# Eight matmuls without a reader, three between gate and up and five between up and w_down

## The chip, the cores and the metric

The kernel runs on one core of one Trainium2 chip. The metric is device time in microseconds (us); a kernel's time is the median of its runs. One more execution is taken with the hardware profiler, and all durations of single instructions come from that one.

## The reference

One decode step of a transformer block for two sequences (B = 2, one token each, D = 640): a modulation of two layer norms by a condition vector, an attention over a cached window, and a gated feed-forward part.

```python
mod = (silu(c) @ w_mod).reshape(2, 6, 1, 640)        # sa, ca, ga, sb, cb, gb
h = layernorm(x) * (1 + ca) + sa
# attention: 32 heads of 192, the last 1024 rows of the caches
q = (h @ wq).reshape(2, 1, 32, 192).transpose(0, 2, 1, 3)
p = softmax(einsum('bhqd,bhkd->bhqk', q, k) * 192 ** -0.5)
o = einsum('bhqk,bhkd->bhqd', p, v)
x = x + ga * (o.transpose(0, 2, 1, 3).reshape(2, 1, 6144) @ wo)
# feed-forward part, F = 1536
h = layernorm(x) * (1 + cb) + sb
return x + gb * ((gelu(h @ w_gate) * (h @ w_up)) @ w_down)
```

All inputs are bf16. The caches and the weights are read once.

## The kernel before

Two rows of activations meet some 77 MB of weights and caches, so the program is one long stream of loads on the SP queue, in an order written out by hand: w_mod, wq, four loads of the key cache, four of the value cache (three places in SBUF hold them in turn), then wo in two pieces, w_gate, w_up and w_down in two pieces of 10 and 2 of its 12 row tiles (`WD_SPLIT`). A load waits only until its place is free.

Every engine gets its instructions as a list in program order. `S.op` and `S.dma` record an operation with what it reads and writes; `emit` writes each list out and puts a semaphore wait before an instruction whose producers run on another engine. TensorE runs its list strictly in that order.

The products with weights are laid out in four column groups: the row block is held as a 128x32 tile, and four matmuls, for the four quarters of the output columns, go to four strips of the array and write to four 32-partition strips of one PSUM bank. So a `wo`, `gate`, `up` or `down` product is a run of matmuls in groups of four: 192 for wo (L577, 128 after the first piece of wo has landed and 64 after the second), 20 each for gate and up (`ffn_gu`, L593), 48 for w_down (L611, 40 and 8 by the two pieces).

The tail of the program, from wo on, is a chain:

- wo (TensorE, L577), its scaling by `ga` and the residual sum (VectorE, L582 and L584);
- the second layer norm (L331 to L354) and the transposition of its result to `hT` (L324);
- `ffn_gu` for gate into bank `BK_G[0]` = 5 (waits for `hT` and w_gate), the gelu on ScalarE (L599);
- `ffn_gu` for up into bank 6 (waits for w_up), the product `geglu` on VectorE (L602), its transposition to `aT` (L324);
- down (TensorE, L611; its first matmul waits for `aT` and the first piece of w_down, its 41st for the second piece);
- the scaling by `gb` and the residual sum (L617, L619), and the store.

`warm(n, bk)` is a helper that the kernel already uses in the scores of the key cache, four matmuls a step (`NF`) into bank 4. It issues `n` matmuls of the 128x128 identity with the 128x384 tile `qbc` (the queries, set early in the program) into a bank that nobody reads afterwards. The first of them (L425) loads the weights, the others (L418, in `held`) keep them:

```python
for i in range(n):
    put = e.matmul if i == 0 else lambda *a, **k: held(e, *a, **k)
    last = put(ps[:, bk, 0:2 * Dh], lhsT=ident_b[:, :], rhs=qbc[:, :, :].rearrange("p b d -> p (b d)"),
               start=True, stop=True)
```

`MB` is (7, 4): the banks of the two halves of the modulation. Bank 7 is read for the last time by the copy of the first half (`mod0_evac`, L372), at the start of the program.

Of the kernel before, what the change touches and what calls it, by code (L numbers as in the profile page):

```python
# [103 lines left out]
def bass_adaLN_cond__sliding_block_cached__geglu_ffn__decode_kernel(  # L104
# [62 lines left out]
    with es:  # L167
# [69 lines left out]
        def bank(k):  # L237
            return ("bank", k)
# [119 lines left out]
        MB = (7, 4)  # L358
# [55 lines left out]
        def held(e, out, lhsT, rhs, start, stop):  # L414
            i = mybir.InstMatmult(name=nc.get_next_instruction_name(), engine=mybir.EngineType.PE,
                                  ins=[e.lower_ap(rhs), e.lower_ap(lhsT)], outs=[e.lower_ap(out)],
                                  start_tensor_calc=start, stop_tensor_calc=stop, tile_size=(P, P), tile_position=(0, 0), ldweights=False)
            return e.add_instruction(i)  # L418

        def warm(n, bk):  # L420
            def f(e):
                last = None
# [4 lines that stand above are left out]
                return last  # L427
            S.op("pe", f, reads=["ident_b", "qbc"], writes=[bank(bk)], name="warm")
# [159 lines left out]
        def ffn_gu(bk, wv, key, name, ka, kb):  # L588
            def f(e):
                last = None  # L590
                for k in range(ka, kb):
                    for j in range(NJ):
                        last = e.matmul(ps[SQ * j:SQ * j + SQ, bk, 0:FN], lhsT=hT[:, k, :], rhs=wv[:, k, FN * j:FN * j + FN],  # L593
                                        start=(k == 0), stop=(k == KT - 1), tile_position=(0, SQ * j), skip_group_check=True)
                return last
            S.op("pe", f, reads=["hT", key], writes=[bank(bk)], name="ffn_" + name)

        ffn_gu(BK_G[0], wg_v, "wg", "wg", 0, KT)
        S.op("act", lambda e: e.activation(out=gl, in_=ps[:, BK_G[0], 0:FN], func=ACTF.Gelu_apprx_tanh),  # L599
             reads=[bank(BK_G[0])], writes=["gl"], name="gelu")  # L600
        ffn_gu(BK_G[1], wu_v, "wu", "wu", 0, KT)
        S.op("dve", lambda e: e.tensor_tensor(out=aC[:, :], in0=ps[:, BK_G[1], 0:FN], in1=gl, op=ALU.mult),  # L602
             reads=[bank(BK_G[1]), "gl"], writes=["aC"], name="geglu")
        to_contraction(aT[:, :, :], aC[:, :], FT, ["aC"], ["aT"], "aT")
# [52 lines left out]
```

## Time and profile before

| | before |
|---|---|
| median of 3 runs | 187.43 us (187.03 to 187.66) |
| profiled execution: time / span | 187.47 us / 186.2 us |
| TensorE matmul busy | 110.8 us (59%), 921 instructions |
| VectorE busy | 101.2 us (54%) |
| load queue's share of the 16 DMA engines | 96.2% |
| read from HBM | 76.88 MB, 413 GB/s over the span |
| mean granted TensorE clock | 0.857 |

The span runs from the first to the last instruction of the profiled execution; 1.27 us of its time lie outside. PE is TensorE's matmuls, PEld its weight loads, DVE is VectorE, ACT ScalarE, SP the engine that issues the loads. The granted clock is the share of full speed that TensorE's throttle let through.

### The profile page before, as it was taken

The numbers are of one execution on the slowest core, as the hardware profiler recorded it, in microseconds if no ns is written. First come the engines' busy times: TensorE is split into PE (matmuls) and PEld (weight loads), VectorE is DVE, ScalarE is ACT, GpSimd is POOL, SyncE is SP. The second block draws the span as 40 slices with busy tenths as digits, with TensorE's granted clock in tenths as the row PEclk, the third lists the DMA queues.
The fourth block names the chain that finished last, engine by engine and source line by source line (L and its number), as shares of the span: only waits on it lengthen the run. The fifth ranks groups of instructions, "written<-read, shape, count | busy, mean of one in ns | idle before, by whom it ended". The sixth has DMA issues, their size and how long they took to land.

```text
span 186.2 us, 1823 instructions
## 1 busy us (share of the span) xinstructions
PE 110.8 (59%) x921; PEld 35.4 (19%) x697; DVE 101.2 (54%) x106; ACT 13.1 (7%) x22; POOL 5.0 (3%) x12
## 2 busy tenths in 40 slices
PE   0004500861089989998899986299759267184333
PEld 0001200330000000000000000256435145183113
DVE  6811500010586999999999994738393601103431
ACT  2002200032000000000000000200100001200300
POOL 8200000000000000000000000000000000000000
PEclk9999999997557999999999999859966969758555
DMA  7999999898998989899998989999898999999980
GB/s 264 396 449 488 475 436 396 348 500 380 465 475 370 487 359 496 370 475 443 412 468 370 496 359 486 412 443 475 363 486 370 465 422 417 418 413 416 426 339 11
DMA packets 2347, 76.99 MB, mean 413 GB/s; under 512 B 292, under 2 KB 292, under 8 KB 420
## 3 DMA queue, kind: packets, MB, share of 16 engines
q1 hardware_dynamic: 2316, 76.88, 96.2%
q8 instruction: 6, 0.10, 0.2%
q10 hardware_dynamic: 24, 0.01, 0.0%
q14 instruction: 1, 0.01, 0.0%
HBM read 76.88 MB, written 0.00 MB: 413 GB/s over the span
## 4 chain that ended last, share of the span: by engine, by line
DMA 44%; DVE 35%; PE 17%; SPq 1%; issue 1%; ACT 0%; DVEq 0%
DMA pp<-in_A_k_cache_dram 25%; DVE pp L432 19%; DMA pp<-in_B_w_down_dram 19%; PE ps L498 12%; DVE r L432 7%; DVE Sg L452 5%; PE ps L418 4%; DVE Em L483 2%; PE ps L611 1%; SPq L252 1%; PE ps L445 1%; DVE On L515 0%; DVE M L458 0%; ACT E_sb L472 0%; PE ps L467 0%
## 5 line engine op out<-in xcount | busy, mean ns | idle before, releaser
L432 DVE TENSOR_TENSOR pp<-pp,qbc 128x6144 bf16<-128x6144 bf16 x12 | 40.1, 3350 | 9.3 <-DMA pp<-in_A_k_cache_dram 9.3
L418 PE MATMUL ps<-pp,ident_b 128*128 128x512 bf16 x132 | 32.8, 400 | 0.0
L498 PE MATMUL ps<-pp,Em 128*64 128x384 bf16 x192 | 23.3, 419 | 9.8 <-DMA pp<-in_A_v_cache_dram 5.1
L483 DVE TENSOR_TENSOR Em<-E_sb,M32b 128x2048 bf16<-128x2048 bf16 x8 | 18.2, 2289 | 8.5 <-PE ps L498 7.8
L498 PEld LDWEIGHTS ps<-pp,Em 128*64 128x64 bf16 x192 | 14.0, 141 | 18.8 <-issue 5.4
L432 DVE TENSOR_TENSOR r<-r,qbc 128x6144 bf16<-128x6144 bf16 x4 | 13.4, 3349 | 0.0
L452 DVE TENSOR_REDUCE Sg<-ps 128x32 f32<-128x512 f32 x16 | 11.0, 685 | 4.4 <-PE ps L418 4.4
L367 PE MATMUL ps<-pp,scT 128*32 128x480 bf16 x40 | 4.4, 601 | 15.0 <-DMA pp<-in_w_mod_dram 15.0
L445 PE MATMUL ps<-pp,ident_b 128*128 128x512 bf16 x12 | 4.9, 407 | 13.4 <-DVE pp L432 13.4
L388 PE MATMUL ps<-r,hT 128*32 128x512 bf16 x60 | 5.5, 545 | 11.5 <-DMA r<-in_A_wq_dram 11.5
L418 PE MATMUL ps<-qbc,ident_b 128*128 128x384 bf16 x48 | 10.6, 330 | 0.0
L418 PE MATMUL ps<-r,ident_b 128*128 128x512 bf16 x44 | 10.1, 379 | 0.0
L399 DVE CAST qC<-ps 128x512 bf16<-128x512 f32 x1 | 0.7, 692 | 16.1 <-PE ps L388 16.1
L577 PE MATMUL ps<-r,oT 128*32 128x160 bf16 x192 | 5.7, 305 | 5.6 <-DMA r<-in_A_wo_dram 5.6
L425 PEld LDWEIGHTS ps<-qbc,ident_b 128*128 128x128 bf16 x16 | 1.6, 101 | 37.7 <-issue 37.7
L515 DVE TENSOR_SCALAR On<-ps,rden 32x192 bf16<-32x192 f32 x4 | 1.7, 418 | 12.4 <-PE ps L498 12.4
L577 PEld LDWEIGHTS ps<-r,oT 128*32 128x32 bf16 x192 | 5.2, 131 | 6.0 <-DMA r<-in_A_wo_dram 6.0
L472 ACT ACTIVATE E_sb<-Sg,nb 128x256 bf16<-128x256 f32 x2 | 1.0, 500 | 74.4 <-DVE nb L470 74.4
L582 DVE TENSOR_TENSOR lnt<-ps,modC 128x160 f32<-128x160 f32 x1 | 0.3, 325 | 10.7 <-PE ps L577 10.7
L593 PE MATMUL ps<-pp,hT 128*32 128x384 bf16 x40 | 3.6, 522 | 3.9 <-DVE hT L324 2.6
L425 PE MATMUL ps<-qbc,ident_b 128*128 128x384 bf16 x16 | 5.4, 338 | 0.7 <-ACT qbc L397 0.7
L445 PEld LDWEIGHTS ps<-pp,ident_b 128*128 128x128 bf16 x12 | 1.2, 97 | 24.4 <-DVE pp L432 23.3
(76 smaller groups left out, 66.0 us busy)
## 6 DMA issues: line engine op xcount, KB each, us to landing
pp<-in_A_k_cache_dram SPq DMA_DIRECT2D x3, 6144.0 KB, 41.4
pp<-in_A_v_cache_dram SPq DMA_DIRECT2D x3, 6144.0 KB, 21.7
r<-in_A_wq_dram SPq DMA_DIRECT2D x1, 7680.0 KB, 31.8
r<-in_A_k_cache_dram SPq DMA_DIRECT2D x1, 6144.0 KB, 38.9
r<-in_A_v_cache_dram SPq DMA_DIRECT2D x1, 6144.0 KB, 22.3
r<-in_A_wo_dram SPq DMA_DIRECT2D x1, 5120.0 KB, 28.7
pp<-in_w_mod_dram SPq DMA_DIRECT2D x1, 4800.0 KB, 14.1
r<-in_A_wo_dram SPq DMA_DIRECT2D x1, 2560.0 KB, 34.4
```

Of the source, the lines that this page charges most:

```text
L252: return lambda e: e.dma_start(dst, src)
L367: last = e.matmul(ps[SQ * j:SQ * j + SQ, bk, 0:3 * DN].rearrange("p (i n) -> p i n", i=3), lhsT=scT[:, k, :], rhs=wm_v[:, k, 3 * part * D: ...
L388: last = e.matmul(ps[SQ * j:SQ * j + SQ, BK_H + c, 0:QW], lhsT=hT[:, k, :], rhs=wq_v[:, k, RN * j + QW * c:RN * j + QW * (c + 1)], start=( ...
L418: return e.add_instruction(i)
L425: last = put(ps[:, bk, 0:2 * Dh], lhsT=ident_b[:, :], rhs=qbc[:, :, :].rearrange("p b d -> p (b d)"), start=True, stop=True)
L432: S.op("dve", lambda e: e.tensor_tensor(out=places[k][:, JH * q:JH * (q + 1), :], in0=places[k][:, JH * q:JH * (q + 1), :], in1=qbc[:, b, ...
L445: last = put(o_ap, lhsT=ident_b[:, :], rhs=places[k][:, JH * q:JH * (q + 1), ci * GC:(ci + 1) * GC], start=(ci == 0), stop=(ci == NCH - 1))
L452: S.op("dve", lambda e: e.tensor_reduce(out=S_sb[:, b, a:a + JH], in_=ps[:, q % 2, 0:JH * GC].rearrange("p (j c) -> p j c", j=JH), axis=AX ...
L483: S.op("dve", lambda e: e.tensor_tensor(out=Em[:, t % 2, :, :], in0=E_sb[:, b, J * t:J * (t + 1)].unsqueeze(2).broadcast_to([P, J, H]), in ...
L498: last = e.matmul(ps[r:r + 2 * H, BK_O[b], 0:ON], lhsT=Em[:, t % 2, 2 * jp:2 * jp + 2, :].rearrange("p j c -> p (j c)"), rhs=places[k][:, ...
L577: last = e.matmul(ps[SQ * j:SQ * j + SQ, BK_M, 0:DN], lhsT=oT[:, t, :], rhs=wo_v[:, t, DN * j:DN * j + DN], start=(t == 0), stop=(t == NT ...
L593: last = e.matmul(ps[SQ * j:SQ * j + SQ, bk, 0:FN], lhsT=hT[:, k, :], rhs=wv[:, k, FN * j:FN * j + FN], start=(k == 0), stop=(k == KT - 1) ...
```

## The change

One `warm` of three matmuls is put behind gate's matmuls and one of five behind up's, both into bank 7.

```diff
         ffn_gu(BK_G[0], wg_v, "wg", "wg", 0, KT)
+        warm(3, MB[0])
         S.op("act", lambda e: e.activation(out=gl, in_=ps[:, BK_G[0], 0:FN], func=ACTF.Gelu_apprx_tanh),
              reads=[bank(BK_G[0])], writes=["gl"], name="gelu")
         ffn_gu(BK_G[1], wu_v, "wu", "wu", 0, KT)
+        warm(5, MB[0])
         S.op("dve", lambda e: e.tensor_tensor(out=aC[:, :], in0=ps[:, BK_G[1], 0:FN], in1=gl, op=ALU.mult),
              reads=[bank(BK_G[1]), "gl"], writes=["aC"], name="geglu")
```

The lines behind it move by one or two (gelu L600, geglu L604, down L613, `gb` L619 and L621).

## The prediction, made before the changed kernel ran

> **What bounds the kernel now.** I read the page first: the row of the granted clock and the chain that ended last.
>
> ```profile
> PEclk9999999997557999999999999859966969758555
> ...
> DMA 44%; DVE 35%; PE 17%; SPq 1%; issue 1%; ACT 0%; DVEq 0%
> ```
>
> The loads run through nearly the whole span, and TensorE stands at half clock (5) in the last three slices, where the change is made. The chain in order of time, of the last 40 us, says what sets the end (start, duration, what):
>
> ```profile
> 146.36 35.41 DMA pp<-in_B_w_down_dram
> 181.78 0.14 issue
> 181.91 1.82 PE ps L611 x47
> ```
>
> The last large load, w_down, lands at 181.78. Behind it come down's matmuls, two small VectorE steps and the store; nothing overlaps them. So of TensorE's work in the tail only down's 1.8 us is on the path. The timeline of TensorE (start, duration, tile, what ended the idle time before) shows what stands ahead of it:
>
> ```profile
> 162.60 4.46 PE L577 MATMUL ps<-r,oT 128*32 128x160 bf16 x128 [3.91 <-DMA r<-in_A_wo_dram]
> 168.71 1.29 PE L577 MATMUL ps<-r,oT 128*32 128x160 bf16 x64 [1.64 <-DMA r<-in_A_wo_dram]
> ...
> 174.83 1.79 PE L593 MATMUL ps<-pp,hT 128*32 128x384 bf16 x20 [2.58 <-DVE hT L324]
> 177.99 1.79 PE L593 MATMUL ps<-pp,hT 128*32 128x384 bf16 x20 [1.37 <-DMA pp<-in_B_w_up_dram]
> 181.91 1.79 PE L611 MATMUL ps<-pp,aT 128*32 128x160 bf16 x48 [2.13 <-DMA pp<-in_B_w_down_dram]
> ```
>
> Gate is followed by a hole of 1.37 us, ended by w_up's landing; up by one of 2.13 us, ended by w_down's. In the second hole VectorE works (whole timeline):
>
> ```profile
> 179.90 0.56 DVE L602 TENSOR_TENSOR aC<-ps,Sg 128x384 bf16<-128x384 f32 x1 [5.13 <-PE ps L593]
> 180.50 0.85 DVE L324 STREAM_TRANSPOSE aT<-aC 128x384 bf16<-128x384 bf16 x1
> ```
>
> aT is done at 181.35, 0.43 us before w_down lands: that is up's slack.
>
> Last, the rule of the clock. In rows of a quarter microsecond it changes at 119.28, 126.08, 143.16, 149.99, 153.40, 160.23, 167.05 and 170.47, always a whole multiple of 3.41 us apart. So I cut the span on that grid (stretch, length, PE busy with its matmuls, granted clock, DMA share, GB/s):
>
> ```profile
> 136.33:139.74 3.41, 2.60 (x18) 0.50 1.07 461
> 139.74:143.16 3.42, 3.42 (x24) 0.50 1.00 431
> ...
> 149.99:153.40 3.41, 2.83 (x18) 0.50 0.97 420
> ...
> 163.64:167.05 3.41, 3.41 (x104) 0.50 0.94 401
> 167.05:170.47 3.42, 1.30 (x68) 1.00 1.01 424
> ...
> 173.88:177.29 3.41, 1.79 (x20) 0.50 1.01 428
> 177.29:180.71 3.42, 1.79 (x20) 0.50 0.90 371
> ```
>
> No stretch is mixed; each decides the clock of the next. A cold stretch with 2.83 us or more of busy TensorE was followed by full clock, one with 2.60 was not. A stretch at full clock with 2.32 or 2.04 kept it (143.16 and 112.43), one with 1.30 lost it. Before the change neither stretch ahead of down comes near: 1.79 and 1.79.
>
> **The change part by part.**
>
> Removed and moved: nothing. The order of the changed kernel's instructions shows ScalarE, VectorE and SP with the same lists, and the eight matmuls (plus two weight loads) on TensorE without a wait: `qbc` and the identity are old, bank 7 was last read near 18 us. gelu and geglu wait for gate's and up's own counts, so no reader waits for the new ones.
>
> Three matmuls behind gate: 384 columns each. Gate's 20 matmuls are five groups of four, 1.79 us with 0.19 us of run-out at the end, so 0.32 us a group; a 128x384 matmul that fills the array should take the same 0.32 us at half clock (L425's and L418's rows, 338 and 330 ns in the mean, mix clocks and run-out). They run from 176.43 to 176.43 + 3 x 0.32 = 177.39, to 177.58 with run-out. Up starts at 177.99. Cover: the wait for w_up, 0.4 us to spare; cost nothing. Their weight load adds between nothing and 0.1 us (L425's PEld, 96 to 151 ns); I take nothing, because at 57.18 the helper's first matmul followed the earlier group without a visible hole. Were the cover gone, up would start up to 0.96 + 0.1 us late, of which up's slack takes 0.43.
>
> Five behind up: from 179.59 for 1.60 us, to 181.19, 181.38 with run-out. down can't start before aT (181.35) and w_down (181.78). This cover doesn't depend on the load: geglu and aT take 1.45 us after up anyway. Cost nothing; bounds 0 and 0.1.
>
> What they do to the clock: the stretch 173.88 to 177.29 gets 174.83 to 177.29 = 2.46 us, under the 2.60 that didn't suffice. The stretch 177.29 to 180.71 gets 0.29 + (180.71 - 177.99) = 3.01 us (2.82 without the run-out in the hole, about the 2.83 that sufficed). So the clock rises at 180.71, before down.
>
> The grid may lie otherwise in another execution, so I ask for every position. Busy blocks are now 174.83 to 177.58 and 177.99 to 181.38. A stretch holds 2.83 us or more if it ends anywhere from 178.07 (start 174.66) to 181.91 (start 178.50). That interval is 3.84 us long, the grid 3.41: some boundary always falls in it, and the clock is up when down starts, unless a further boundary takes it back (second rival).
>
> The Trainium skill, "TensorE: Matmul & The Clock Gate", Part 1 ("What's actually happening"), calls the window free-running and not reset by a kernel's start; the grid above agrees on its length (3.41 us), and the one trace can't show whether it moves between executions.
>
> What a full clock saves: wo gives both prices for the same matmul (128x32 weights, 160 columns). At half clock 32 groups took 4.46 us: (4.46 - 0.19)/32 = 0.133 us a group. At full clock 16 groups took 1.29: (1.29 - 0.17)/16 = 0.070. down is 12 groups: cold 12 x 0.133 + 0.19 = 1.79, as its row says; warm 12 x 0.070 + 0.17 = 1.01. Saved: 0.78 us, all on the path. Bounds are 0 (no rise) and 0.78. The second piece of w_down doesn't become the new wait: the DMA share is 0.07 of an engine set at 182.0 to 182.1 and nothing by 182.2, and a warm down needs it after 181.91 + 10 x 0.070 = 182.61.
>
> Up running faster, where the clock rises early, gains nothing: w_down still lands at 181.78.
>
> Sum: 187.47 - 0.78 = 186.69 us. The profiled execution is 0.04 above the median of the runs.
>
> **The rivals.**
>
> *The clock doesn't rise in time: no change, 187.4.* For it: the margin is thin, 3.01 or 2.82 against a threshold between 2.60 and 2.83, and a hole between gate's matmuls and the helper's (their weight load) would take another 0.1. Against: two of the readings reach a level at which it did rise. The Trainium skill's same page and part (table of the two states) asks for a whole window of sustained activity, some 3.4 us; by it the longest unbroken block, 177.99 to 181.38 = 3.39 us, falls just short and the saving is 0. The row at 149.99 speaks against this reading: 2.83 of 3.41 us sufficed.
>
> *The clock rises early and falls back: between 186.7 and 187.4.* If a boundary lies between 178.07 and 179.6, up and the helper run at double pace (0.80 + 0.80 + 0.19 us), TensorE then stands still to 181.91, and the next boundary comes at 181.48 to 183.0, before or in down. That stretch holds some 1.8 us busy, between the 1.30 that lost the clock and the 2.04 that kept it. 1.5 of 3.41 positions are concerned; in a bit under half of these I expect a loss, of half the gain in the mean.
>
> *The three matmuls hold up back: slower, 188.1.* If gate ends later against w_up's landing (wo's last 64 matmuls at half clock would make it 16 x 0.063 = 1.0 us later), the three start at 177.43 and end at 178.39, up starts 0.4 late, which the 0.43 of slack just takes. It costs time from where gate is more than 1.0 us late, and in full (1.06 - 0.43 = 0.63 us) only where w_up and w_down both have landed before; and then the clock mustn't rise either. 187.47 + 0.63 = 188.1. The 1.37 us hole with DMA as its end speaks against it.
>
> **How the numbers follow.** Forecast 0.66, no rise 0.15, fall back 0.10, held back 0.06, the rest 0.03. About 0.3% (0.56 us) is what a measurement of this kernel tells from no change, so the forecast, 0.4%, counts as faster, mostly; a part of it measured short of 0.3% is set off by falls back that keep most of the gain. Faster 0.66; same takes the first two rivals, 0.25; slower the third and part of the rest, 0.09. The runs before spread by 0.4 us to either side of their median, so the forecast's own range is 186.3 to 187.1. The whole range must reach the case of no change: 186.2 to 187.5, which leaves the slower case out.
>
> **What would show it.** Right: in the profile after, three and five matmuls end before up and down start, up still waits for w_up and down for w_down at the same times, the clock reads 1.00 through down, and the 48 matmuls take about 1.0 us in place of 1.79. Wrong: down at 1.79 us with the clock at 0.50 (no rise), down with a change of pace inside (fall back), up starting at the end of the three matmuls (held back), or a down that is fast while the end doesn't come earlier.

## The result

The changed kernel takes 186.88 us (median of 13 runs, 186.72 to 187.36) against 187.51 (13 runs, 186.81 to 187.81): ratio 0.997, 95% interval 0.996 to 0.998. That is 0.63 us, just over the 0.3% (0.56 us) that can be told from no change. The profiled execution took 186.95 us with a span of 185.7, against 187.47 and 186.2.

First TensorE's part of the timeline of the changed kernel (start, duration, engine, line, tile; what ended the idle time before):

```profile
168.77 2.32 PE L577 MATMUL ps<-r,oT 128*32 128x160 bf16 x64 [1.64 <-DMA r<-in_A_wo_dram]
...
175.93 1.79 PE L593 MATMUL ps<-pp,hT 128*32 128x384 bf16 x20 [2.58 <-DVE hT L324]
177.66 0.50 PE L425 MATMUL ps<-qbc,ident_b 128*128 128x384 bf16 x1
177.95 0.85 PE L418 MATMUL ps<-qbc,ident_b 128*128 128x384 bf16 x2
178.73 1.79 PE L593 MATMUL ps<-pp,hT 128*32 128x384 bf16 x20
180.45 0.50 PE L425 MATMUL ps<-qbc,ident_b 128*128 128x384 bf16 x1
180.74 1.35 PE L418 MATMUL ps<-qbc,ident_b 128*128 128x384 bf16 x4
182.15 1.01 PE L613 MATMUL ps<-pp,aT 128*32 128x160 bf16 x48
```

down's 48 matmuls take 1.01 us, before 1.79. But up starts at 178.73, before at 177.99, and without a wait for a load: it starts where the three helpers end. wo's last 64 matmuls took 2.32 us here, before 1.29. The chain that ended last shows the consequence: it no longer goes through w_down's landing.

```profile
177.72 0.43 PE ps L425
178.16 0.64 PE ps L418 x2
178.80 1.75 PE ps L593 x12
...
181.24 0.87 DVE aT L324
182.11 0.04 issue
182.15 1.04 PE ps L613 x48
```

Two of the helpers' rows and up are links of the chain now, and down waits for aT (182.10). Cut at this execution's own clock boundaries (stretch, length, PE busy, granted clock, DMA share, GB/s):

```profile
175.00:178.42 3.42, 2.49 (x23) 0.50 1.00 425
178.42:181.83 3.41, 3.41 (x27) 0.50 0.69 277
181.83:185.24 3.41, 1.28 (x50) 1.00 0.01 5
```

The grid lies elsewhere than before (181.83 against 180.71). The stretch of up and the five is wholly busy, and the clock rises 0.32 us ahead of down.

The sum of this execution: 0.78 us won in down, 182.15 - 181.91 = 0.24 lost in its later start, 0.54 in all; the two profiled times differ by 0.52.

The single runs of before say more than their median. For 78 of them, made beside the experiments below, the mean granted clock of each run is on record. In 67 it is 0.855 to 0.872, and all of these take 187.24 us or more; in the other 11 it is 0.874 to 0.883, and they take 186.51 to 187.36. So before, too, some executions seem to reach the time of the changed kernel, with a higher clock. None of these was profiled, so that down ran at full clock in them is not shown.

### The profile page after: what moved, and what is told of

It reads as the page before. It is cut to its first block, busy times and chain, and to the rows that moved or that the text cites. A ratio compares the mean times of both kernels' runs of the same rounds, so it can differ in the third digit from the quotient of the medians.

```text
span 185.7 us, 1833 instructions
## 1 busy us (share of the span) xinstructions
PE 110.3 (59%) x929; PEld 35.9 (19%) x699; DVE 101.4 (55%) x106; ACT 13.1 (7%) x22; POOL 4.8 (3%) x12
## 4 chain that ended last, share of the span: by engine, by line
DMA 45%; DVE 36%; PE 16%; issue 1%; SPq 1%; ACT 0%; DVEq 0%
DMA pp<-in_A_k_cache_dram 25%; DMA r<-in_A_wo_dram 19%; DVE pp L432 19%; DVE r L432 7%; PE ps L498 7%; DVE Sg L452 5%; PE ps L418 4%; PE ps L593 2%; PE ps L577 1%; DVE Em L483 1%; SPq L252 1%; PE ps L613 1%; PE ps L445 1%; DVE aT L324 0%; DVE M L458 0%
## 5 line engine op out<-in xcount | busy, mean ns | idle before, releaser
L418 PE MATMUL ps<-pp,ident_b 128*128 128x512 bf16 x132 | 32.0, 393 | 0.0
L498 PE MATMUL ps<-pp,Em 128*64 128x384 bf16 x192 | 20.2, 379 | 14.2 <-DMA pp<-in_A_v_cache_dram 12.9
L367 PE MATMUL ps<-pp,scT 128*32 128x480 bf16 x40 | 4.4, 601 | 15.1 <-DMA pp<-in_w_mod_dram 15.1
L388 PE MATMUL ps<-r,hT 128*32 128x512 bf16 x60 | 6.0, 586 | 11.5 <-DMA r<-in_A_wq_dram 11.5
L418 PE MATMUL ps<-qbc,ident_b 128*128 128x384 bf16 x54 | 12.6, 346 | 0.0
L445 PE MATMUL ps<-pp,ident_b 128*128 128x512 bf16 x12 | 4.9, 407 | 12.8 <-DVE pp L432 12.8
L577 PE MATMUL ps<-r,oT 128*32 128x160 bf16 x192 | 6.8, 339 | 5.1 <-DMA r<-in_A_wo_dram 5.1
L577 PEld LDWEIGHTS ps<-r,oT 128*32 128x32 bf16 x192 | 6.1, 146 | 5.5 <-DMA r<-in_A_wo_dram 5.5
L425 PE MATMUL ps<-qbc,ident_b 128*128 128x384 bf16 x18 | 6.2, 345 | 0.7 <-ACT qbc L397 0.7
L388 PEld LDWEIGHTS ps<-r,hT 128*32 128x32 bf16 x60 | 2.4, 140 | 15.4 <-issue 15.3
```

The lines of the kernel that those rows point to most:

```text
L367: last = e.matmul(ps[SQ * j:SQ * j + SQ, bk, 0:3 * DN].rearrange("p (i n) -> p i n", i=3), lhsT=scT[:, k, :], rhs=wm_v[:, k, 3 * part * D: ...
L388: last = e.matmul(ps[SQ * j:SQ * j + SQ, BK_H + c, 0:QW], lhsT=hT[:, k, :], rhs=wq_v[:, k, RN * j + QW * c:RN * j + QW * (c + 1)], start=( ...
L445: last = put(o_ap, lhsT=ident_b[:, :], rhs=places[k][:, JH * q:JH * (q + 1), ci * GC:(ci + 1) * GC], start=(ci == 0), stop=(ci == NCH - 1))
L498: last = e.matmul(ps[r:r + 2 * H, BK_O[b], 0:ON], lhsT=Em[:, t % 2, 2 * jp:2 * jp + 2, :].rearrange("p j c -> p (j c)"), rhs=places[k][:, ...
L577: last = e.matmul(ps[SQ * j:SQ * j + SQ, BK_M, 0:DN], lhsT=oT[:, t, :], rhs=wo_v[:, t, DN * j:DN * j + DN], start=(t == 0), stop=(t == NT ...
```

## The experiments

Theory 1: TensorE's clock for a stretch of 3.41 us is set by how long it was busy in the stretch before; the eight matmuls lift that over a threshold. Theory 2: all that counts is that TensorE is busy right ahead of down. Theory 3: the three hold up back in some executions and cost part of the gain. Runs of one group below share their runs of before.

**One half of the change at a time**

```diff
-        warm(3, MB[0])      # five_only
-        warm(5, MB[0])      # three_only
```

> The three matmuls behind gate are left out, the five behind up stay. Theory 1 (the clock): a stretch of the 3.41 us grid must hold about 2.83 us of busy TensorE. The block from 177.99 to 181.38 is then alone, and a stretch must end between 180.82 and 181.91 to have down at full clock from its start: a third of all positions. Where it ends up to 1 us later, a part of down is fast; in the other third there is no gain. So times scatter between 186.7 and 187.5, the mean gains 0.3 to 0.45 us, less than the change's 0.63. Theory 2 (what counts is only that TensorE is busy right ahead of down): the whole 0.63 us, as with all eight, and no more scatter.

> The five behind up are left out, the three behind gate stay. Theory 1: gate, three and up give at most 2.75 + a part of 1.79 in a row, so for some positions a stretch from about 174.7 to 178.1 or 176 to 179.8 rises, but then TensorE stands still from 179.8 to 181.9 and the clock may fall back: mean gain 0 to 0.2, median about 0. Theory 2: no gain. Theory 3 (the three hold up back by up to 0.7 us where wo's second part runs at half clock, as the profile of the changed kernel shows): up to 0.3 us slower than before in those executions.

The five alone: 186.79 us, ratio 0.9978 (0.9964 to 0.9992). The twelve runs fall in two groups: eight from 186.53 to 186.90, four from 187.22 to 187.55; the mean gains 0.50 us (187.46 before, 30 runs), more than the 0.3 to 0.45 expected. Theory 2, which expects no more scatter than the change has, does not fit these four; what decides against it is a profile shown further down (as_changed). The mean granted clock of each run parts the groups as well: 0.878 to 0.890 in the eight, 0.863 to 0.872 in the four. (One stretch of 3.41 us at full instead of half clock makes 0.009 of a span of 186 us.) The profiled execution is of the good group, and its windows show why:

```profile
177.53:180.95 3.42, 3.19 (x25) 0.50 0.86 351
180.95:184.36 3.41, 1.24 (x49) 1.00 0.10 38
```

The boundary at 180.95 lies in the interval that the expectation named (180.82 to 181.91). The other group wasn't profiled; that its boundaries lie outside is argued, not shown. Eight good runs of twelve are also more than the third of all positions that the expectation gave them: it took every position for equally likely.

The three alone: 187.40 us, ratio 0.9989 (0.9974 to 1.0004), so not told from no change; the mean gains 0.20. Three of the twelve runs, at 186.64 to 186.74, are as fast as the change, which theory 1 allows for some positions; none of them was profiled. The profiled execution shows theory 3 without the gain:

```profile
178.67 1.79 PE L593 MATMUL ps<-pp,hT 128*32 128x384 bf16 x20
182.07 1.79 PE L612 MATMUL ps<-pp,aT 128*32 128x160 bf16 x48 [1.62 <-DVE aT L324]
```

Up starts at 178.67, behind the three, and down, at half clock, waits for aT to 182.07. The stretch ahead held too little for a rise (175.10 to 178.51: 2.64 us busy). This execution took 187.68 us, 0.16 over the median before.

**The same matmuls, a quarter of the array; and the change again**

```diff
-        warm(3, MB[0])
+        strip(3, MB[0])
...
-        warm(5, MB[0])
+        strip(5, MB[0])
# strip: each matmul with lhsT=ident_b[:, 0:SQ], out=ps[0:SQ, bk, 0:2 * Dh], tile_position=(0, 0)
```

> The same eight matmuls at the same places, 128x384 each, but with only 32 of the 128 columns of the weights, so that each fills one of four strips of the array and takes the same 0.32 us at half clock. Theory 1a (the clock follows the time that TensorE is busy): the gain of the change, 0.63 us, down at about 1.0 us. Theory 1b (it follows how much of the array works): the eight count a quarter, the stretches hold at most 1.8 + 0.4 us, down stays at 1.79 us, and the time is that of before or up to 0.3 us over it, where the three hold up back. This would also be the control for theory 2, which expects the gain of 0.63.

> The changed kernel once more, on the chip of the three others: 186.9 us, a gain of 0.6 us. Its profile shows another position of the clock's grid: if that is free against the kernel's start, the boundaries lie elsewhere than at 178.42 and 181.83. Where wo's last 64 matmuls take 1.3 us, up starts by w_up's landing near 178.0 and down by w_down's; where they take 2.3, up starts at the end of the three, near 178.7, and down by aT, near 182.1.

one_strip takes 186.69 us (7 runs, 186.62 to 186.75), ratio 0.9962 (0.9948 to 0.9977): the full gain, as theory 1a has it and 1b does not. A second profile of the same kernel (strip_again, below) shows the stretch ahead of the rise:

```profile
177.23:180.64 3.41, 3.08 (x26) 0.50 0.94 386
```

Up's 1.79 us are in it; the other 1.29 are strip matmuls alone. Counted as a quarter these would give 1.79 + 0.32 = 2.11 us, and no stretch at half clock with so little was followed by full clock. So the clock follows the time in which TensorE is busy, also where its matmuls use 32 of 128 columns.

The change again: 186.81 us (12 runs, 186.57 to 187.04), ratio 0.9968 (0.9957 to 0.9979). Its windows, and down:

```profile
175.43:178.84 3.41, 2.76 (x23) 0.50 0.99 420
178.84:182.26 3.42, 2.19 (x42) 1.00 0.57 224
...
182.03 1.02 PE L613 MATMUL ps<-pp,aT 128*32 128x160 bf16 x48 [1.23 <-DMA pp<-in_B_w_down_dram]
```

2.76 us sufficed. It is also the case that decides against theory 2: from 180.79 TensorE stood still for 1.23 us, waiting for w_down, and down still took 1.02.

The profiled execution of one_strip has the slow wo (2.33 us) too, and yet:

```profile
177.51 0.85 PE L434 MATMUL ps<-qbc,ident_b 128*32 128x384 bf16 x2
177.95 0.51 PE L602 MATMUL ps<-pp,hT 128*32 128x384 bf16 x3
178.15 0.53 PE L434 MATMUL ps<-qbc,ident_b 128*32 128x384 bf16 x1
178.25 1.34 PE L602 MATMUL ps<-pp,hT 128*32 128x384 bf16 x17
...
181.89 1.01 PE L622 MATMUL ps<-pp,aT 128*32 128x160 bf16 x48 [1.49 <-DMA pp<-in_B_w_down_dram]
```

L434 is the helper in one strip, L602 is up. Up's first matmuls start at 177.95, beside the helper in its one strip, not behind it, and down again starts by w_down's landing (181.89). This is the one profile of the strip with the slow wo.

**How much the covers hold**

```diff
-        warm(3, MB[0])
+        warm(6, MB[0])      # six_five
...
-        warm(5, MB[0])
+        warm(10, MB[0])     # three_ten
```

> Six matmuls behind gate in place of three, five behind up as in the change. The clock rises as surely as with eight (a stretch can't miss the block), so a theory without a price for holding up back expects the change's gain, 0.6 us, or a little more. Cover theory: at half clock the six take 1.92 us. Where wo's second part was fast (gate ends 176.4), up starts at 178.4, inside its slack; where it was slow (gate ends near 177.5), up starts at about 179.4 and aT ends near 182.8, 0.9 us behind w_down, which takes the whole gain back. So scatter from 186.7 to 187.8 and a mean gain of about 0.3 to 0.45.

> Three behind gate, ten behind up. At half clock ten would end at 179.6 + 3.2 = 182.8, 0.9 us after w_down has landed. But the clock rises between 178.1 and 181.9, and what is left of the ten then runs at 0.16 us each: they end between 181.2 and 182.5. Cover theory: gain 0.4 to 0.6 in the mean, single runs up to 0.5 us worse than the change. If the cover by geglu and aT were not what hides the five, ten would cost 1.6 us more than five at half clock: 188.0.

Six: 186.79 us, ratio 0.9972 (0.9952 to 0.9991), eight of nine runs at 186.67 to 187.03 and one at 188.26; mean gain 0.47. In the profiled execution wo was fast, and up started at 178.65, behind the helpers (178.4 was expected); the clock rose at 180.26 and down started at 182.08, after a wait for aT. So in most executions six cost little; the 188.26 is of the size of the cover theory's worst case but wasn't profiled.

Ten: 186.81 us in the median, ratio 0.9972 (0.9952 to 0.9991), but three of eight runs at 187.23 to 187.91, mean gain 0.39. The profiled execution is one of these:

```profile
180.64 0.50 PE L425 MATMUL ps<-qbc,ident_b 128*128 128x384 bf16 x1
180.93 2.26 PE L418 MATMUL ps<-qbc,ident_b 128*128 128x384 bf16 x9
183.12 1.01 PE L613 MATMUL ps<-pp,aT 128*32 128x160 bf16 x48
...
175.38:178.79 3.41, 2.67 (x23) 0.50 1.01 426
```

down starts without any idle time at 183.12, when the last helper has ended: 0.85 us after aT (182.27, with up held back by the three as well), more than its fast clock wins. The clock rose only at 182.21 here; the stretch ahead of up had held 2.67 us (175.38 to 178.79), which did not suffice. Nor did 2.69 in wo_four (173.90 to 177.32), while as_changed's 2.76 did: in the tail the threshold lies between these two. Earlier in the program it does not. In stretches with the matmuls of the value cache, 2.60 of the profile before did not suffice, while 2.61 of strip_again and 2.62 of strip_wo (149.87 to 153.28) did; strip_again's rows:

```profile
136.27:139.68 3.41, 2.61 (x18) 0.50 1.03 447
139.68:143.09 3.41, 3.41 (x46) 1.00 1.07 461
```

So the busy time, as the profile counts it, gives no one threshold to 0.1 us. What else counts isn't shown.

**Other holes filled**

```diff
             S.op("pe", f, reads=[("wo", i), "oT"], writes=[bank(BK_M)], name="wo%d" % i)
+            if i == 0:
+                warm(4, MB[0])      # wo_four
...
         layer_norm("ln2", 1, 3)
+        warm(7, MB[0])              # ln_seven
```

> The change, and four more matmuls between the two parts of wo, in the hole of 1.64 us that ends with the landing of wo's second piece. wo's last 64 matmuls then run at full clock in nearly every execution (1.3 us, not 2.3), gate ends near 176.4 and the three are out of up's way: up starts by w_up's landing. If the three's holding back is what costs the change the 0.1 to 0.15 us between its 0.63 to 0.7 and the 0.78 of down alone, this gives 186.7. Rival: the clock now rises earlier, TensorE's work in the tail is done sooner, and the clock falls back before down in more positions: mean gain under 0.6, some runs at 187.4.

> The change, and seven more matmuls behind the layer norm's statistics (L335), in the hole of 2.6 us before gate. The busy block then begins 2.6 us earlier: the clock rises before or in gate in most positions, gate and the three take half the time, and up is not held back whatever wo's pace: 186.7, with less scatter than the change. Rival, as before: early rise, then 2 us without work ahead of down (from 179.9 to 181.9), and a fall back for some positions: some runs at 187.4.

wo_four: 186.78 us, ratio 0.9964 (0.9946 to 0.9982), 7 runs to 186.89. In its profile up starts by w_up's landing (177.88, after 0.39 us of waiting) and down by w_down's (181.81). That execution's grid would have made wo fast anyway, so it doesn't show that the four did it. But it shows the case that the prediction worked out, a fast wo and a boundary at 180.73, with the change's eight matmuls in their places:

```profile
177.32:180.73 3.41, 3.02 (x25) 0.50 0.91 375
```

The prediction had 3.01 us for this stretch; the clock rose at its end, and down took 1.01.

ln_seven: 186.82 us, ratio 0.9964 (0.9952 to 0.9976), 10 runs to 187.05; the clock rose at 177.10 and stayed, with 2.45 us busy in the next stretch, and down took 1.01 us behind 2.02 without work. Neither can be told from the change.

**The strip again, and everything together**

strip_again is one_strip unchanged; strip_wo adds `strip(4, MB[0])` between wo's parts; all_holes is the change with wo_four's and ln_seven's additions at once.

> one_strip once more. Its profile showed up's first matmuls starting beside the helper's third, which occupies one of four strips, at 177.95, where the full-width helper held them to 178.7 to 178.9. If that is what made it 0.1 us faster than the change (186.69 against 186.81), it comes out at 186.65 to 186.75 again with no run above 186.9; if the difference was chance, near 186.8 with the change's scatter up to 187.0.

> one_strip, with four more one-strip matmuls between the two parts of wo. Both things that let up start late are gone. If holding up back is all that was left, this is not faster than one_strip (186.65 to 186.75), since there up already starts in time. If the pace of wo still counts, 186.6 or under. Rival: an early rise and a fall back, single runs at 187.4.

> The change with both additions at once: four between the two parts of wo, seven behind the layer norm's statistics. Filling theory (more busy time is always safer): 186.7 with the least scatter. Fall-back theory: with the clock already full in gate and up, the work of the tail takes half its time, the holes grow (0.9 us busy of gate, 0.5 of the three, 0.9 of up, 0.8 of the five in 7 us), a stretch can hold 1.4 to 1.7 us, and the clock can be lost ahead of down: some runs at 187.3 to 187.5.

> all_holes once more, since its profile was of an execution in which TensorE ran far under its usual pace throughout, and its other five executions (186.82 to 187.26) were slower than the change's although their mean clock was higher (0.876 to 0.903 against 0.868 to 0.889). Fall-back theory: a grid stretch that ends between 181.4 and 183 holds under the 1.7 us or so that keep the clock, and down's groups change from 0.070 to 0.133 us inside or ahead of down; executions spread between 186.7 and 187.5. If instead down runs at full clock and starts later than 181.9, it is the loads or the chain ahead of it.

strip_again: 186.70 us (5 runs, 186.58 to 186.79), ratio 0.9954 (0.9942 to 0.9967). strip_wo: 186.74, ratio 0.9960 (0.9946 to 0.9974): nothing more to win there. All twelve runs of the strip are at or under 186.79; of the 25 runs of the change 16 are over that, up to 187.36. But strip_wo, with the same strip matmuls and four more, has two of its five runs at 186.92 and 186.95, and the intervals of the ratios overlap. So the strip looks better by its scatter and by some 0.1 us of median, not by a separated interval. That its place beside up is the reason isn't shown either: in strip_again's profile wo was fast and up started by w_up's landing.

all_holes: ratio 0.9973 (0.9960 to 0.9985) and, the second time, 186.78 us and 0.9967 (0.9952 to 0.9983). One execution took 580.16 us, with TensorE slow from start to end; it is left out of the ratio and is told of at the end (the five others of the first time: 187.07 in the median). Of the other 17 runs three are at 187.26, 187.31 and 187.78, where the change has one of 25 over 187.2. More filling didn't help. The second profile is of a good execution (up by w_up's landing at 177.96, down by w_down's at 181.90, 1.01 us), so whether the slower runs lost the clock or started down late stays open.

## Why the prediction was right, point by point

- **What sets the end**: right, with one exception. In as_changed, one_strip and five_only down waits for w_down as before; in the first profile of the change it waited for aT and started 0.24 us later than before. That profile shows at once what the prediction named as a sign of being right (full clock through down) and one that it named as a sign of being wrong (up starting at the end of the three).
- **The price of a full clock**: 0.78 us, right. down takes 1.01 or 1.02 us at full clock in every profile that has it, 1.79 at half.
- **The clock rises before down at every position of the grid**: right where it was seen, not shown for every position. The two profiles of the change rose at 181.83 and 178.84, which are 0.42 us apart on the grid; wo_four's rose at 180.73, at the position of the forecast. No run of the change is over 187.36, but that run, near the time of before, wasn't profiled. The nearest miss is three_ten's grid: its stretch to 178.79, with the same matmuls as the change up to there, held too little, and the next boundary is at 182.21, hardly before the change's down could have started there (aT at 182.27). The threshold was put between 2.60 and 2.83 us; the tails of the runs have 2.69 to 2.76. (The prediction's list of the clock's changes leaves out one, at 136.33, on the same grid.) The Trainium skill's "TensorE: Matmul & The Clock Gate", Part 1, table of the two states, asks for a whole sustained window, some 3.4 us; 2.76 of 3.41 sufficed here, so the measurement decides against that reading. What the same part says of a window that runs free of the kernel agrees: the changes of the clock lie on multiples of 3.41 us inside each profile, but at 180.71 in the one of before and 181.83 in the one after.
- **The three are free**: the step that failed. Priced with wo fast, they had 0.4 us to spare, and wo_four, where wo was fast, shows 0.39. The third rival had them 0.4 us in up's way with wo slow, inside its slack of 0.43. The first profile of the change has 0.74: wo and gate were 1.10 us late instead of 1.0, the helper started 1.73 us after gate's first matmul instead of 1.60, and up started 1.07 us after the helper's first instead of 0.96. So 0.13 and 0.11 us were lost at the two seams of the helper; the text had named one such hole, of up to 0.1, as a bound and taken it at nothing, because the row at 57.18 showed none. No hole shows in the timeline here either: the helper starts at 177.66, before gate's end at 177.72. Only the times from one start to the next tell it. aT came at 182.10, 0.75 us later than before, and down 0.24 later. That accounts for the profiled execution. The forecast, 186.69, is 0.19 under the median after; with wo slow it would have been 186.69 + 0.24 = 186.93, the profiled 186.95. In as_changed wo was slow as well, but the clock rose at 178.84, up took 1.00 us, and down waited for w_down again.
- **What every position leaves out**: the prediction moved the grid and kept wo fast. The two go together. In the eight profiles with a boundary between 180.26 and 180.95 (the one of before among them) wo's second part took 1.29 us; in the five with one between 181.83 and 182.26 it took 2.32 or 2.33. None of these 13 (the execution of 580 us left aside) has one between 180.95 and 181.83 or between 182.26 and 183.67, so the positions are not evenly spread.
- **The five are free**: right, but barely. In the profiled execution they end at 182.09, aT at 182.10. Ten are not free.
- **Fall back**: not seen in a profile. as_changed is the rival's own case, with a rise between 178.07 and 179.6: its next stretch held 2.19 us, where the rival had some 1.8, and the clock stayed. one_strip's held 1.93, and it stayed too. In all_holes, which would favour a fall back, it stays open.

## What to carry to other kernels

Work that no one reads can pay where a short burst of matmuls stands alone on the path behind a load: what must be bought is busy time in the clock's stretch ahead (here 2.76 of 3.41 us was enough and 2.69 was not), and its price is what it holds up at half clock. Ask for every position of the clock's grid, since one profile shows one position and the kernel's earlier stages move with it too (wo's second part at 1.29 or 2.32 us). A filler that uses one strip of the array bought the same clock here, and in one_strip's profile the real matmuls started beside it.

## What was not expected of the hardware

- The clock counts one-strip matmuls as busy time: with 1.29 of its 3.08 us from them, a stretch of strip_again was followed by full clock. At half their length the stretch would hold 2.44 us, less than any that was followed by it.
- Losing the clock doesn't take a long pause: in the profile before, the stretch from 167.05 to 170.47 held 1.30 us of work and no pause over 1.64 us, and the next was at half clock. ln_seven lost it with 1.34; one_strip kept it with 1.93 (178.73 to 182.15). Between these the busy time alone doesn't decide: the changed kernel kept the clock with 1.39 (134.04 to 137.45), all_holes_2 lost it with 1.54 (170.31 to 173.72).
- One execution of all_holes took 580.16 us. In its page the matmuls of the key scores, 400 ns in the mean before, took 1708, and the first matmuls of the program (L367) 1529 in place of 601. The mean granted clock of the execution is given as 1.00 all the same; its page has no row of the clock. The row of the key scores:

```profile
L418 PE MATMUL ps<-pp,ident_b 128*128 128x512 bf16 x132 | 178.9, 1708 | 0.0
```

  The other 17 runs of that kernel show nothing like it, and no run here tells its cause.
